# Turn-back of head pairs moved into the next period, one-hots of heads 3 to 11 placed by DMA, and a re-laid opening, in a routed-attention plus feed-forward kernel

## The chip, the cores and the metric

The kernel runs on one core of a Trainium2 chip. Times are device microseconds (us) of one execution. Kernels are compared only within the same rounds. A run that lies over 1.5% above the fastest of its kernel is called slow and left out.

## The reference

Attention in which a query sees only the keys that were assigned to the same one of 16 centroids, and then a feed-forward block without a nonlinearity:

```python
# B, H, S, D = 4, 8, 768, 64; 16 centroids per head
q_assign = argmax(normalise(q) @ normalise(centroids).T)      # k_assign likewise
mask     = q_assign[:, :, :, None] == k_assign[:, :, None, :]
scores   = where(mask, q @ k.T / 8, -1e9)
x        = softmax(scores) @ v                                # to [3072, 512]
out      = ((x @ w1) * (x @ w2)) @ w3 @ w_out
# ... (types, draws and reshapes cut)
```

## The kernel before

There are 32 heads (batch times head), each with its own *period*. Period p computes the scores and exponentials of head p, the value products of head p-1, and the preparation of head p+2. What is to be done in a period is a list of pairs (position, item), sorted by position and issued in that order; every engine then works through its own queue in order. Feed-forward work ("fill") is spread between these items. The kernel multiplies w3 by w_out once, so the fill has two kinds of products: up (`pu`) and down (`po`).

*Routing* of a head (`prr`) gives centroid scores, from which VectorE makes one-hots (`oh`). The one-hots are then transposed into PSUM (`pso`) and copied, 16 partitions at a time, into rows 64 to 79 of the head's transposed q and k (`xqk`), so that the score product applies the mask by itself. *Turn-back* (`join`): when both heads of a pair are done, their output (`xtm`) is transposed into PSUM (`psx`) and copied to `xT_all`, the feed-forward's input.

```python
psum_sc = tile_pool(name="psum_sc", bufs=3, space=PSUM)
psum_av = tile_pool(name="psum_av", bufs=1, space=PSUM)
psum_r  = tile_pool(name="psum_r",  bufs=1, space=PSUM)     # prr, pso, psx, pct: one bank in turn
psum_f  = tile_pool(name="psum_f",  bufs=3, space=PSUM)     # pst, pw, pu, po
# ...
    def route_turn(g, qeng=None):
        def item():
            pso = psum_r.tile([P, 3, P], BF16, name="pso", tag="r")
            for r in range(3):
                nc.tensor.transpose(out=pso[:, r], in_=oh[:, r]..., identity=ident)
            for a in (2, 0, 3, 1):
                dst = xqk[D : D + C, 3 * a : 3 * a + 3, :]
                src = pso[32 * a : 32 * a + C]
                # a < 2: a copy (VectorE, or qeng); else VectorE: src * MASKB - MASKB
# ...
    def join(g):
        xtm = xtm_cur[0]
        def item():
            psx = psum_r.tile([P, NCH, P], BF16, name="psx", tag="r")
            for sub in range(NCH):
                nc.tensor.transpose(out=psx[:, sub], in_=xtm[:, sub], identity=ident)
            nc.vector.tensor_copy(out=xT_all[:, h // 2, b * S : (b + 1) * S], in_=psx...)
# ...
        if 1 <= p and p + 2 < NG:
            work += [(0.36, route(p + 2)), (0.68, route_turn(p + 2))]
        if p >= 1:
            work += [(0.23 + 0.13 * i, it) for i, it in enumerate(av_items(p - 1))]
        if p >= 1 and (p - 1) % H % 2 == 1:
            work += [(0.93, lambda: join(p - 1)())]
# ...
        if p >= 1 and p % H == 0:      # a batch is complete: release its feed-forward items
```

The softmax here doesn't subtract the row's maximum and nothing guards it: scores larger than these inputs give would overflow.

## Time and profile before

| | before |
|---|---|
| median of the timed runs | 314.77 us (313.33 to 316.89) |
| span of the profiled run | 310.5 us |
| TensorE, ScalarE, VectorE, GpSimd busy | 92%, 66%, 59%, 34% |
| TensorE's waits of the turn-back on one-hot copies | 9.3 us in 14 waits |
| first score product | 15.04 us after the start |

In a timeline a line is: start, duration, engine, line, operation, what it writes and reads, count, and in brackets how long the engine had been idle and what ended it. The opening is seen in the following lines of the timeline of the kernel before (one-hots of head 0):

```profile
12.44 0.35 DVE L355 TENSOR_SCALAR xqk<-pso 16x384 bf16<-16x384 bf16 x1 [0.60 <-PE pso L343]
...
12.89 0.47 ACT L351 COPY xqk<-pso 16x384 bf16<-16x384 bf16 x1 [1.32 <-DVE xqk L355]
...
13.39 0.36 DVE L355 TENSOR_SCALAR xqk<-pso 16x384 bf16<-16x384 bf16 x1 [0.59 <-ACT xqk L351]
...
13.79 0.47 ACT L351 COPY xqk<-pso 16x384 bf16<-16x384 bf16 x1 [0.43 <-DVE xqk L355]
```

VectorE and ScalarE take turns on one bank; each starts when the other has ended.

### The profile page before, as it was taken

The page shows a single profiled execution, that of the slowest core. Times are in us where ns is not written, and L with a number is a line of the kernel's source. Part 1 is how long each engine was busy: PE and PEld are TensorE (multiplying, and loading weights), DVE is VectorE, ACT ScalarE, POOL GpSimd, SP SyncE. Part 2 cuts the span into 40 slices and gives each one's busy share as a digit, 9 for nine tenths or more (in the row PEclk, how much of TensorE's full clock was granted, in tenths as well). Part 3 has the DMA queues.
Part 4 walks back from the last instruction along what each step waited for, and adds up shares of the span by engine and source line. Part 5 has one row for each costly group of instructions (what it writes and reads, how often), then busy time and mean ns, then how long its engine had stood idle before and what let it go on. Part 6 is the DMA issues. An engine that isn't in the chain of part 4 may idle for free.

```text
span 310.5 us, 7304 instructions
## 1 busy us (share of the span) xinstructions
PE 286.6 (92%) x2972; PEld 172.1 (55%) x2972; DVE 183.6 (59%) x420; ACT 204.6 (66%) x369; POOL 104.7 (34%) x120
## 2 busy tenths in 40 slices
PE   5589898989799999999899999999999998999994
PEld 1447676655465656655565655555555555444441
DVE  4678798757676677655765465655666622342421
ACT  5667888755478888788677676867677776332330
POOL 1899875412633343073461047330300000000000
PEclk9657999999999999999999999999999999999999
DMA  7999997407555730879930689603910011002103
GB/s 188 290 252 229 264 261 170 70 0 141 141 137 135 148 106 0 173 196 229 199 106 12 162 222 225 158 0 100 243 25 2 1 70 68 2 0 101 36 0 136
DMA packets 52209, 38.78 MB, mean 125 GB/s; under 512 B 33744, under 2 KB 47056, under 8 KB 52176
## 3 DMA queue, kind: packets, MB, share of 16 engines
q1 hardware_dynamic: 48640, 32.88, 41.5%
q0 software_dynamic: 3392, 5.24, 9.9%
q8 instruction: 23, 0.38, 0.5%
q10 hardware_dynamic: 144, 0.20, 0.2%
q14 instruction: 10, 0.08, 0.1%
HBM read 29.39 MB, written 6.29 MB: 115 GB/s over the span
## 4 chain that ended last, share of the span: by engine, by line
PE 75%; DVE 13%; DMA 4%; ACT 3%; issue 2%; SPq 1%; DVEq 0%; ACTq 0%
PE pu L220 23%; PE po L239 13%; PE av L407 10%; PE sc L375 10%; PE sc L385 6%; PE pw L195 4%; DVE xqk L355 4%; DVE xqk L353 4%; PE prr L320 3%; PE psx L439 3%; PE pst L305 2%; DMA x_130<-in_k_dram 2%; DMA xqk<-stg 2%; PE pso L343 1%; ACT ex L379 1%
## 5 line engine op out<-in xcount | busy, mean ns | idle before, releaser
L379 ACT ACTIVATE ex<-sc 128x512 bf16<-128x512 f32 x192 | 111.8, 601 | 37.2 <-PE sc L375 36.2
L375 PE MATMUL sc<-xqk 80*128 80x512 bf16 x192 | 71.6, 390 | 0.3 <-ACT ex L379 0.2
L389 ACT ACTIVATE ex<-sc 128x512 bf16<-128x512 f32 x96 | 57.6, 600 | 19.6 <-PE sc L385 19.0
L228 DVE TENSOR_TENSOR ab<-pu,asb 128x512 bf16<-128x512 f32 x48 | 33.2, 692 | 42.5 <-PE pu L220 34.6
L407 PEld LDWEIGHTS <-ex 128*128 128x128 bf16 x1152 | 46.1, 98 | 10.3 <-ACT ex L379 0.4
L220 PE MATMUL pu<-xT_all,w1b 128*128 128x512 bf16 x192 | 49.4, 378 | 0.0
L220 PE MATMUL pu<-xT_all,w2b 128*128 128x512 bf16 x192 | 49.3, 378 | 0.0
L239 PE MATMUL po<-wc,ab 128*128 128x512 bf16 x192 | 47.0, 378 | 0.0
L226 ACT CAST asb<-pu 128x512 bf16<-128x512 f32 x48 | 28.1, 586 | 27.0 <-PE pu L220 26.8
L385 PE MATMUL sc<-xqk 80*128 80x256 bf16 x192 | 37.7, 278 | 0.4 <-ACT ex L389 0.2
L324 DVE TENSOR_REDUCE rsc<-prr 128x192 f32<-128x384 f32 x32 | 17.7, 554 | 27.1 <-PE prr L320 27.1
L239 PEld LDWEIGHTS <-ab 128*128 128x128 bf16 x192 | 18.5, 97 | 18.9
L220 PEld LDWEIGHTS <-w2b 128*128 128x128 bf16 x192 | 18.5, 97 | 18.8 <-issue 0.3
L220 PEld LDWEIGHTS <-w1b 128*128 128x128 bf16 x192 | 18.4, 97 | 18.5
L355 DVE TENSOR_SCALAR xqk<-pso 16x384 bf16<-16x384 bf16 x64 | 22.9, 358 | 5.3 <-PE pso L343 3.5
L385 PEld LDWEIGHTS <-xqk 80*128 80x128 bf16 x192 | 16.9, 100 | 13.2 <-issue 2.1
L353 DVE COPY xqk<-pso 16x384 bf16<-16x384 bf16 x62 | 21.7, 350 | 0.9
L375 PEld LDWEIGHTS <-xqk 80*128 80x128 bf16 x192 | 18.3, 99 | 6.4
L320 PEld LDWEIGHTS <-xqk 128*128 128x128 bf16 x384 | 14.8, 97 | 7.3 <-DVE xqk L309 1.8
L420 DVE TENSOR_TENSOR xtm<-av,rcp 128x384 bf16<-128x384 f32 x32 | 17.8, 558 | 1.1
L439 PE MATMUL psx<-ident,xtm 128*128 128x128 bf16 x96 | 8.1, 221 | 10.2 <-DVE xqk L353 9.3
L247 DVE COPY osb<-po 128x512 f32<-128x512 f32 x12 | 8.3, 692 | 15.4 <-PE po L239 15.2
(173 smaller groups left out, 348.5 us busy)
## 6 DMA issues: line engine op xcount, KB each, us to landing
out_dram<-osb SPq DMA_DIRECT2D x24, 256.0 KB, 2.1
w3b<-in_moe_w_dram POOLq DMA_DIRECT2D x8, 256.0 KB, 6.7
wob<-in_moe_w_out_dram POOLq DMA_DIRECT2D x4, 256.0 KB, 8.0
w1b<-in_moe_w_dram POOLq DMA_DIRECT2D x4, 256.0 KB, 6.6
w2b<-in_moe_w_dram POOLq DMA_DIRECT2D x4, 256.0 KB, 4.8
xqk<-stg SPq DMA_TRANSPOSE x20, 4.1
x_126<-in_q_dram ACTq DMA_DIRECT2D x1, 192.0 KB, 2.6
x_126<-in_k_dram SPq DMA_DIRECT2D x1, 192.0 KB, 2.7
```

The source lines that it names most:

```text
L220: nc.tensor.matmul(pu, lhsT=wb[:, fc, jc * P : (jc + 1) * P], rhs=xT_all[:, fc, t0 : t0 + TB], start=(fc == 0), stop=(fc == 3),)
L226: nc.scalar.copy(out=st["a"], in_=pu)
L228: nc.vector.tensor_tensor(out=st["ab"][:, jc], in0=pu, in1=st.pop("a"), op=ALU.mult)
L239: nc.tensor.matmul(st["o"], lhsT=st["ab"][:, jc, sub * P : (sub + 1) * P], rhs=wc[:, jc], start=(jc == 0), stop=(jc == 7),)
L320: nc.tensor.matmul(prr[:, j], lhsT=st["xqk"][:, j, :], rhs=cnt2[:, g % H], start=True, stop=True)
L353: nc.vector.tensor_copy(out=dst, in_=src)
L355: nc.vector.tensor_scalar(out=dst, in0=src, scalar1=MASKB, scalar2=-MASKB, op0=ALU.mult, op1=ALU.add,)
L375: nc.tensor.matmul(sc, lhsT=xqk[0:KR, NCH + 2 * pr + part, :], rhs=xqk[0:KR, 0:4, :], start=True, stop=True,)
L379: nc.scalar.activation(out=ex[:, part, 0:512], in_=sc, func=ACT.Exp, scale=SM_SCALE)
L385: nc.tensor.matmul(sc[:, i], lhsT=xqk[0:KR, NCH + 2 * pr + i, :], rhs=xqk[0:KR, 4:6, :], start=True, stop=True,)
L389: nc.scalar.activation(out=ex[:, :, 512:S], in_=sc, func=ACT.Exp, scale=SM_SCALE)
L407: nc.tensor.matmul(st["av"][:, sub, 0:VCOL], lhsT=st["exs"][j // 2][:, j % 2, sub * P : (sub + 1) * P], rhs=st["vb"][:, j, 0:VCOL], start= ...
```

## The change

Its intent: take the wait of the turn-back away by moving it to the next period, where the one-hot copies are long over; relieve VectorE of three of four copies for heads 3 to 11; and let the opening run through with a shorter chain, two banks for head 0's one-hots and a warmer TensorE.

```diff
-        for last in (False, True):          # two steps of the square root, now one
+        # ... one step (cut)
-        nc.scalar.copy(out=cnsrc[:, 1, D:P], in_=hi)
+        nc.vector.tensor_scalar_mul(out=cnsrc[:, 1, D:P], in0=cen, scalar1=rden)
 # cen_turn: its two transposes now in banks of psum_r and psum_f (cut)
+    def route_turn(g, split=False):
+        def direct():                       # head 0: split, two PSUM tiles, ScalarE beside VectorE
+            pso = ones_up(g, psum_r, "r")
+            psq = ones_up(g, psum_f, "f") if split else pso
+            # ... the four copies as before
+        def by_dma():
+            pso = ones_up(g, psum_r, "r")
+            ohT = rtp.tile([P, 3, P], BF16, name="ohT")
+            nc.vector.tensor_scalar(out=ohT, in0=pso, scalar1=msc[:, 0:1], scalar2=msc[:, 1:2],
+                                    op0=ALU.mult, op1=ALU.add)
+            for a in range(4):
+                nc.sync.dma_start(ones_rows(g, a), ohT[32 * a : 32 * a + C])
+        return by_dma if 3 <= g < PE_HEADS else direct
-        warm_up(10)
+        warm_up(13)
 # begin: order of cen_turn, turn_pe and low changed (cut)
-        route_turn(0, nc.scalar)()
+        warm_up(6)
+        route_turn(0, True)()
-            work += [(0.10, turn_pe(p + 2, 0)), (0.20, turn_pe(p + 2, 1))]
+            work += [(0.06, turn_pe(p + 2, 0)), (0.16, turn_pe(p + 2, 1))]
-            work += [(0.36, route(p + 2)), (0.68, route_turn(p + 2))]
+            work += [(0.45, route(p + 2)), (0.90, route_turn(p + 2))]
-        if p >= 1 and (p - 1) % H % 2 == 1:
-            work += [(0.93, lambda: join(p - 1)())]
+        if p % 2 == 1 and p >= 3:
+            work += [(0.25, join(p - 2))]
+        if p == NG:
+            work += [(0.95, join(p - 1))]
-        if p >= 1 and p % H == 0:
+        if (p > 1 and p % H == 1) or p == NG:
```

The last line follows from the move: a batch is complete one period later, so its feed-forward items are released one period later.

More of the change, by code (lines that the diff above doesn't have):

```diff
@@ L113 @@
     ident = const.tile([P, P], BF16, name="ident")
+    msc = const.tile([P, 2], F32, name="msc")
     ohs = [const.tile([P, 3, 4, 32], BF16, name=f"oh{i}") for i in range(3)]
@@ L124, in constants @@
             nc.vector.memset(oh, 0.0)
+        nc.vector.memset(msc[0 : P // 2, 0:1], 1.0)
+        nc.vector.memset(msc[0 : P // 2, 1:2], 0.0)
+        nc.vector.memset(msc[P // 2 : P, 0:1], MASKB)
+        nc.vector.memset(msc[P // 2 : P, 1:2], -MASKB)
         for vb in vbs:
@@ L136, in cen_norm @@
         nc.scalar.sqrt(nrm, ss)
-        for last in (False, True):
-            rr = setup.tile([P, 1], F32, name="rr")
-            nc.vector.reciprocal(out=rr, in_=nrm)
-            nrm2 = setup.tile([P, 1], F32, name="nrm2")
-            nc.vector.scalar_tensor_tensor(
-                out=nrm2, in0=ss, scalar=rr, in1=nrm, op0=ALU.mult, op1=ALU.add
-            )
-            nrm = setup.tile([P, 1], F32, name="nrm3")
-            nc.vector.tensor_scalar(
-                out=nrm, in0=nrm2, scalar1=0.5, scalar2=(1e-6 if last else 0.0),
-                op0=ALU.mult, op1=ALU.add,
-            )
+        rr = setup.tile([P, 1], F32, name="rr")
+        nc.vector.reciprocal(out=rr, in_=nrm)
+        twice = setup.tile([P, 1], F32, name="twice")
+        nc.vector.scalar_tensor_tensor(
+            out=twice, in0=ss, scalar=rr, in1=nrm, op0=ALU.mult, op1=ALU.add
+        )
+        den = setup.tile([P, 1], F32, name="den")
+        nc.vector.tensor_scalar(
+            out=den, in0=twice, scalar1=0.5, scalar2=1e-6, op0=ALU.mult, op1=ALU.add
+        )
         rden = setup.tile([P, 1], F32, name="rden")
-        nc.vector.reciprocal(out=rden, in_=nrm)
+        nc.vector.reciprocal(out=rden, in_=den)
         hi = cnsrc[:, 0, 0:D]
         nc.vector.tensor_scalar_mul(out=hi, in0=cen, scalar1=rden)
-        nc.scalar.copy(out=cnsrc[:, 1, D:P], in_=hi)
+        nc.vector.tensor_scalar_mul(out=cnsrc[:, 1, D:P], in0=cen, scalar1=rden)
         nc.vector.scalar_tensor_tensor(
@@ L161, in cen_turn @@
     def cen_turn():
-        pct = psum_r.tile([P, 2, P], BF16, name="pct", tag="r")
         for which in range(2):
-            nc.tensor.transpose(out=pct[:, which], in_=cnsrc[:, which, :], identity=ident)
-        for which in range(2):
+            pool, tag = ((psum_r, "r"), (psum_f, "f"))[which]
+            pct = pool.tile([P, P], BF16, name="pct", tag=tag)
+            nc.tensor.transpose(out=pct, in_=cnsrc[:, which, :], identity=ident)
             (nc.vector.tensor_copy, nc.scalar.copy)[which](
-                out=cnt2[:, :, :, which],
-                in_=pct[:, which].rearrange("p (h c) -> p h c", c=C),
+                out=cnt2[:, :, :, which], in_=pct.rearrange("p (h c) -> p h c", c=C)
             )
@@ L335, in route, with ones_up @@
         return item
-    def route_turn(g: int, qeng=None):
-        def item():
-            xqk = state[g]["xqk"]
-            oh = ohs[g % len(ohs)]
-            pso = psum_r.tile([P, 3, P], BF16, name="pso", tag="r")
-            for r in range(3):
-                nc.tensor.transpose(
-                    out=pso[:, r], in_=oh[:, r].rearrange("p a c -> p (a c)"), identity=ident
-                )
+    def ones_up(g: int, pool, tag):
+        oh = ohs[g % len(ohs)]
+        pso = pool.tile([P, 3, P], BF16, name="pso", tag=tag)
+        for r in range(3):
+            nc.tensor.transpose(
+                out=pso[:, r], in_=oh[:, r].rearrange("p a c -> p (a c)"), identity=ident
+            )
+        return pso
@@ L346, in item, with ones_rows, route_turn @@
+    def ones_rows(g: int, a: int):
+        return state[g]["xqk"][D : D + C, 3 * a : 3 * a + 3, :]
+    def route_turn(g: int, split: bool = False):
+        def direct():
+            pso = ones_up(g, psum_r, "r")
+            psq = ones_up(g, psum_f, "f") if split else pso
             for a in (2, 0, 3, 1):
-                dst = xqk[D : D + C, 3 * a : 3 * a + 3, :]
-                src = pso[32 * a : 32 * a + C]
                 if a < 2:
-                    if qeng is nc.scalar:
-                        nc.scalar.copy(out=dst, in_=src)
-                    else:
-                        nc.vector.tensor_copy(out=dst, in_=src)
+                    (nc.scalar.copy if split else nc.vector.tensor_copy)(
+                        out=ones_rows(g, a), in_=psq[32 * a : 32 * a + C]
+                    )
@@ L354, in item @@
                 else:
                     nc.vector.tensor_scalar(
-                        out=dst, in0=src, scalar1=MASKB, scalar2=-MASKB,
-                        op0=ALU.mult, op1=ALU.add,
-                    )
-        return item
+                        out=ones_rows(g, a), in0=pso[32 * a : 32 * a + C],
+                        scalar1=MASKB, scalar2=-MASKB, op0=ALU.mult, op1=ALU.add,
+                    )
+        def by_dma():
+            pso = ones_up(g, psum_r, "r")
+            ohT = rtp.tile([P, 3, P], BF16, name="ohT")
+            nc.vector.tensor_scalar(
+                out=ohT, in0=pso, scalar1=msc[:, 0:1], scalar2=msc[:, 1:2], op0=ALU.mult, op1=ALU.add
+            )
+            for a in range(4):
+                nc.sync.dma_start(ones_rows(g, a), ohT[32 * a : 32 * a + C])
@@ L393, in score_items @@
         return [item(pr, part) for pr in range(NCH // 2) for part in range(3)]
-    xtm_cur = {}
+    xtms = {}
     def av_items(g: int):
@@ L418, in it @@
                     if h % 2 == 0:
-                        xtm_cur[0] = xtmp.tile([P, NCH, P], BF16, name="xtm")
+                        xtms[g + 1] = xtmp.tile([P, NCH, P], BF16, name="xtm")
                     nc.vector.tensor_tensor(
-                        out=xtm_cur[0][:, :, (h % 2) * D : (h % 2) * D + D],
+                        out=xtms[g | 1][:, :, (h % 2) * D : (h % 2) * D + D],
                         in0=av[:, :, 0:D],
@@ L433, in join @@
         b, h = g // H, g % H
-        xtm = xtm_cur[0]
         def item():
+            xtm = xtms.pop(g)
             psx = psum_r.tile([P, NCH, P], BF16, name="psx", tag="r")
@@ L471, in begin @@
         low(0, 0, nc.vector)
+        cen_turn()
+        turn_pe(0, 0, "a")()
         low(0, 1, nc.vector)
-        turn_pe(0, 0, "a")()
-        cen_turn()
-        turn_pe(0, 1, "va")()
+        turn_pe(0, 1)()
         nc.scalar.activation(out=warm[:, 0:1], in_=warm[:, 0:1], func=ACT.Exp)
@@ L518, in in_period @@
         elif p == 1:
-            work += [(0.05, route_turn(2))]
+            work += [(0.02, route_turn(2))]
         if 1 <= p and p + 2 < PE_HEADS:
-            work += [(0.10, turn_pe(p + 2, 0)), (0.20, turn_pe(p + 2, 1))]
+            work += [(0.06, turn_pe(p + 2, 0)), (0.16, turn_pe(p + 2, 1))]
         if 1 <= p and p + 2 < NG:
-            work += [(0.36, route(p + 2)), (0.68, route_turn(p + 2))]
+            work += [(0.45, route(p + 2)), (0.90, route_turn(p + 2))]
         if p >= 1:
             work += [(0.23 + 0.13 * i, it) for i, it in enumerate(av_items(p - 1))]
-        if p >= 1 and (p - 1) % H % 2 == 1:
-            work += [(0.93, lambda: join(p - 1)())]
+        if p % 2 == 1 and p >= 3:
+            work += [(0.25, join(p - 2))]
+        if p == NG:
+            work += [(0.95, join(p - 1))]
         n = FILL(p, len(fill))
```

## The prediction

> **What bounds the kernel now.** I read the totals by engine first, then the waits, then the timeline around the longest wait of TensorE, then the busy times by stage. Totals, waits and transfer landings (a wait line is total us, times, longest):
>
> ```profile
> PE 286.6 (92%) x2972; PEld 172.1 (55%) x2972; DVE 183.6 (59%) x420; ACT 204.6 (66%) x369; POOL 104.7 (34%) x120
> ...
> PEld L439 <- DVE xqk L353: 15.8, 14, 2.1
> ...
> PE psx L439 <- DVE xqk L353: 9.3, 14, 1.7
> ...
> xqk<-stg SPq DMA_TRANSPOSE x20, 4.1
> ...
> cen<-in_centroids_dram SPq DMA_DIRECT2D x1, 32.0 KB, 2.4
> ```
>
> TensorE is busy for 92% of 310.5 us, so only 24 us of idle can be won. One cause holds 9.3 us of it: 14 times the transposes that turn a finished pair of heads back (psx) wait for VectorE to empty the one-hots (pso), because both use the single PSUM buffer of the routing pool. One such wait, from the timeline late in the kernel (start, duration, instruction, idle before it):
>
> ```profile
> 203.47 0.35 DVE L355 TENSOR_SCALAR xqk<-pso 16x384 bf16<-16x384 bf16 x1
> ...
> 203.84 0.35 DVE L353 COPY xqk<-pso 16x384 bf16<-16x384 bf16 x1
> 203.95 0.38 PE L375 MATMUL sc<-xqk 80*128 80x512 bf16 x1
> ...
> 204.20 0.36 DVE L355 TENSOR_SCALAR xqk<-pso 16x384 bf16<-16x384 bf16 x1
> 204.57 0.35 DVE L353 COPY xqk<-pso 16x384 bf16<-16x384 bf16 x1
> ...
> 204.98 0.34 PEld L439 LDWEIGHTS <-xtm 128*128 128x128 bf16 x6 [1.15 <-DVE xqk L353]
> 204.98 0.51 PE L439 MATMUL psx<-ident,xtm 128*128 128x128 bf16 x6 [0.65 <-DVE xqk L353]
> ```
>
> Four copies of 0.35 us run one after another and end at 204.92; psx starts 0.06 us later, after 0.65 us of idle TensorE. Busy times by stage (a period is the work between the first score products of two heads; the rows are heads 0, 1, 2, 3, and 24, 25):
>
> ```profile
> 15.04:22.86 7.82, 6.40 (x49) 3.64 (x46) 5.75 (x12) 4.83 (x9) 7.65 (x11) 0.50 1.00 249
> 22.86:29.57 6.71, 6.70 (x85) 5.09 (x84) 5.30 (x14) 4.01 (x8) 6.54 (x10) 0.71 1.00 213
> 29.57:36.46 6.89, 5.72 (x89) 4.10 (x89) 5.66 (x15) 6.05 (x11) 6.80 (x9) 1.00 1.13 275
> 36.46:42.01 5.55, 5.50 (x93) 4.32 (x91) 4.79 (x10) 4.43 (x10) 4.49 (x6) 1.00 1.17 264
> ...
> 197.34:206.41 9.07, 8.42 (x90) 4.97 (x89) 5.29 (x13) 7.03 (x13) 3.09 (x3) 1.00 0.17 56
> 206.41:214.32 7.91, 7.91 (x85) 4.72 (x84) 4.74 (x11) 5.55 (x10) 0.69 (x1) 1.00 0.10 35
> ```
>
> The columns are length, then busy time and count of PE, PEld, DVE, ACT, POOL, then granted clock, DMA share, GB/s. Even heads carry the turn-back and last longer (9.07 against 7.91, 6.89 against 5.55). In the odd ones TensorE is never idle, so they show the period that is left when the wait goes. The first two periods ran at half clock (0.50, 0.71), and DMA was at its full share up to head 3.
>
> **What the Trainium skill says.** "TensorE: Matmul & The Clock Gate", Part 1 (the HAM clock gate): the clock is halved until a free-running window of about 3.4 us was busy, and drops after an idle one. The trace agrees: the ten opening products come at 0.427 us each (512 columns at half rate), the clock record turns to 1.0 at 6.4 us, back to 0.5 at 9.8 and to 1.0 at 26.9. "PSUM — Partial Sum Buffer", bank collisions: two engines must not touch one bank and quadrant at once, so readers of one bank must be ordered. In the trace ScalarE and VectorE take turns on head 0's one-hots (12.44, 12.89, 13.39, 13.79), four copies in 1.82 us. "VectorE: DVE Perf Modes", errata section: a PSUM source costs 120 cycles plus the elements over the speed-up at 0.96 GHz, whatever the partitions; for 384 bf16 at 2x that is 0.33 us; the trace has 0.35 to 0.36 us for 16 x 384 and for 128 x 384. So one 128-partition copy costs what one 16-partition copy does. "DMA: Bandwidth & Descriptors", anatomy of one DMA: about 2 us are fixed; the smallest transfer here (32 KB) landed in 2.4 us.
>
> **The change, part by part.**
>
> 1. *Turn-back moved.* psx goes from position 0.93 of an even period to 0.25 of the next odd one, and the one-hots from 0.68 to 0.90. Between one-hots and psx there now lie, late in the kernel, two products groups of 0.86 us, three score products of 0.22 and one sixth of the values (0.41): 2.8 us. The four copies need about 0.5 + 1.42 = 1.9 us. The wait should vanish. Its worth: 9.3 us of recorded idle, and a bit more, since the end of a busy block includes the pipeline's tail. Late even minus odd is 9.07 - 7.91 = 1.16 us; the six transposes themselves take 0.34 (their weight loads), so the wait really cost 0.82 where 0.65 is recorded. 14 x 0.17 = 2.4; together 11.7 us. With only three fill items in periods 10 to 16 the distance is about 1.9 us, which is marginal; I take off 1.0. **-10.7.**
> 2. *One-hots of heads 3 to 11 by DMA.* Nine times four copies (1.42 us) become one copy (0.36) and four transfers: 9 x 1.06 = 9.5 us less on VectorE, which does not bound; worth nothing by itself. The cost is a new latency. Copy and wait 1.0 us, four issues at some 0.4 us = 1.6, landing 2.4: 5.0 to 5.8 us, against 1.1 periods to the head's first product, 6.1 us at 5.5 us per period. It just fits; for heads 3, 4, 5 and 10 (whose periods are short) I allow a little. The queue is in order, so loads of inputs from head 6 on now also wait for these transfers: head 6's load moves from 15 us to about 28, needed prepared at about 37, with 3 us to land and 3 us of GpSimd (0.84 + 1.64 + 0.50): hidden by some 3 us. **+0.7.**
> 3. *Opening.* One square-root step less (0.16 + 0.22 + 0.15 and gaps, 0.64 us), the centroid copy off ScalarE, the one-hots of head 0 in two banks (saves about 0.9). Against it, six warming products ahead of head 0's one-hots: 6 x 0.427 = 2.6 us at half clock, starting about 9.7, done 12.2, while the one-hots should be ready at 11.4. And head 1's two copies, not head 0's, released the first score product at 15.04. Net **-0.4**.
> 4. *Clock.* 13 + 6 warming products should bring the full clock at some 13 us instead of 26.9. Heads 0 and 1 at full clock would last some 6.3 (then VectorE's chain, 5.75 busy) and 5.6 us: -2.2. But the window's phase is not ours; I take two thirds: **-1.5.**
> 5. *Fill moved.* The product work of a batch is released one period later: period 9 gets none, period 31 gets 5 instead of 2. Period 9 keeps about 4.9 us of TensorE work against nine exponentials at about 0.5 us: little lost, **+0.3**. In period 31 TensorE waited on exponentials (0.22 + 0.29 us idle) and is now covered: **-0.5.** The wait of the last turn-back (0.9 us) stays.
>
> Sum: -10.7 + 0.7 - 0.4 - 1.5 + 0.3 - 0.5 = -12.1. From the median of 315.3: **303.2 us**.
>
> **Rivals.** (a) *The DMA of the one-hots comes late*, and the head's first score product waits in place of psx. For it: DMA share is 1.0 until 42 us, transfers of 192 KB took 6 to 8 us to land there, 5.8 against 6.1 us is no margin. Against: input loads are now held back, so their queue is empty by then. Up to 9 waits of 1 us: 312 us. (b) *ScalarE becomes the bound early.* For it: 6.05 of 6.89 us in head 2. Against: its records overlap (0.60 us each, 0.5 apart), odd head 3 with the same work lasts 5.55. It would take 2 us of the gain: 305. (c) *Input loads held by the in-order queue* starve GpSimd's preparation in heads 4 to 8: a few us, 306 to 308. (d) *The clock stays at half* and the six warming products only delay: +0.9 + 1.5, 305.6.
>
> **Range and chances.** The main term is firm, as odd periods already run without the wait; (a) and (c) can eat half, the clock can give 1 more. The three runs before differ by 3.6 us. Range 298.5 to 309; the 2% line is at 309.0. Faster 0.88, same 0.10, slower 0.02.
>
> **What would show it.** Right: no wait of psx on VectorE beyond the last one; even and odd late periods 8.1 and 8.2 us, equal within 0.3; the granted clock at 1.0 from some 13 us; the first score product at 14.6; the first products of heads 3 to 11 not waiting for DMA. Wrong: a row in which score weights or products wait for the one-hot transfers or the turn-back still waits for the pso copies; half clock up to 25 us; preparation on GpSimd waiting for inputs in heads 6 to 8 and TensorE waiting for it; the even and odd periods equal but both nearer 9 us, which would mean that the wait had hidden something else.

## The result, and the profile after

The changed kernel takes 304.77 us at the median (303.42 to 306.23), against 314.77. The ratio is 0.968, 95% interval 0.959 to 0.976. Such a ratio is the mean time of one kernel's fast runs over that of the other's of the same rounds, so it is not quite the ratio of the medians. The prediction had 303.2 us. The result is correct.

The totals and the remaining waits of the turn-back (psx), from the page and the waits of the kernel after:

```profile
PE 283.5 (93%) x2948; PEld 172.8 (57%) x2984; DVE 178.0 (59%) x395; ACT 202.1 (66%) x367; POOL 103.4 (34%) x120
...
PE psx L456 <- DVE xqk L359: 1.6, 3, 0.6
...
PE psx L456 <- DVE xtm L437: 1.2, 1, 1.2
...
PE pwarm L471 <- ACT warm L493: 1.1, 1, 1.1
...
PEld L392 <- DMA xqk<-ohT: 0.5, 1, 0.5
```

Fourteen waits of 9.3 us in all became three of 1.6 us in all. (Of the 2984 matmuls that the weight loads count, 36 have no record here, so TensorE's 283.5 us are a little low.) Two new lines have appeared: the warming products waited for ScalarE, and a head's scores for a transfer of one-hots. Late in the kernel the timeline shows what was intended:

```profile
198.31 0.36 DVE L363 TENSOR_SCALAR xqk<-pso 16x384 bf16<-16x384 bf16 x1
198.68 0.35 DVE L359 COPY xqk<-pso 16x384 bf16<-16x384 bf16 x1
...
199.71 0.35 PEld L456 LDWEIGHTS <-xtm 128*128 128x128 bf16 x6
199.74 0.50 PE L456 MATMUL psx<-ident,xtm 128*128 128x128 bf16 x6
```

The last copy ends at 199.03; psx comes 0.71 us later, with no idle in brackets. The stages, with the same columns as in the prediction; heads 0, 1, 2, 3, and 25, 26:

```profile
16.68:24.71 8.03, 5.20 (x48) 3.32 (x45) 6.13 (x12) 4.73 (x9) 7.86 (x11) 0.79 0.70 117
24.71:30.07 5.36, 5.10 (x87) 4.03 (x84) 4.57 (x12) 4.02 (x8) 3.83 (x5) 1.00 0.82 135
30.07:35.10 5.03, 4.92 (x84) 3.98 (x83) 3.90 (x10) 4.73 (x10) 0.00 (x0) 1.00 0.43 77
35.10:41.49 6.39, 5.78 (x97) 4.71 (x97) 4.31 (x11) 5.64 (x11) 4.33 (x5) 1.00 0.62 186
198.06:206.30 8.24, 8.18 (x90) 5.06 (x90) 6.08 (x14) 6.44 (x13) 5.39 (x5) 1.00 0.39 104
206.30:214.20 7.90, 7.84 (x83) 4.71 (x83) 4.47 (x11) 6.00 (x11) 0.51 (x1) 1.00 0.10 36
```

The late pair takes 16.14 us instead of 16.98. Its two periods differ by 0.34 us, the six transposes. But the first row begins at 16.68: the first score product comes 1.64 us later than before, although the opening was meant to be shorter. These are two single executions; the table below has more of each opening.

### The profile page after: what moved, and what is told of

Same layout as the page of the kernel before. It is cut to its first block, busy times and chain, and to the rows that moved or that the text cites.

```text
span 304.2 us, 7357 instructions
## 1 busy us (share of the span) xinstructions
PE 283.5 (93%) x2948; PEld 172.8 (57%) x2984; DVE 178.0 (59%) x395; ACT 202.1 (66%) x367; POOL 103.4 (34%) x120
## 4 chain that ended last, share of the span: by engine, by line
PE 80%; DVE 8%; ACT 5%; DMA 4%; issue 2%; SPq 0%; DVEq 0%
PE pu L223 25%; PE po L242 13%; PE sc L392 12%; PE av L424 11%; PE sc L402 5%; PE pw L198 4%; PE prr L323 3%; ACT ex L396 2%; DMA x<-in_q_dram 2%; DVE oh L331 2%; PE pst L308 2%; PE psx L456 2%; PE pso L344 2%; DMA xqk<-ohT 1%; ACT ex L406 1%
## 5 line engine op out<-in xcount | busy, mean ns | idle before, releaser
L424 PEld LDWEIGHTS <-ex 128*128 128x128 bf16 x1152 | 47.0, 97 | 13.5 <-issue 1.5
L424 PE MATMUL av<-vb,ex 128*128 128x65 bf16 x1152 | 51.7, 193 | 0.2
L291 POOL TENSOR_TENSOR stg<-x,stg 128x768 bf16<-128x768 f32 x30 | 49.4, 1646 | 2.5
L290 POOL CAST stg<-x 128x768 bf16<-128x768 f32 x30 | 24.9, 832 | 72.4 <-DMA x<-in_k_dram 50.9
L223 PE MATMUL pu<-xT_all,w1b 128*128 128x512 bf16 x179 | 47.4, 378 | 0.7
L223 PE MATMUL pu<-xT_all,w2b 128*128 128x512 bf16 x183 | 47.5, 378 | 0.5
L242 PE MATMUL po<-wc,ab 128*128 128x512 bf16 x184 | 45.1, 378 | 0.4
L285 POOL CAST vb<-x 128x384 bf16<-128x384 f32 x32 | 16.7, 521 | 32.1 <-PE av L424 24.9
L402 PEld LDWEIGHTS <-xqk 80*128 80x128 bf16 x192 | 16.9, 98 | 11.0 <-issue 0.5
L363 DVE TENSOR_SCALAR xqk<-pso 16x384 bf16<-16x384 bf16 x46 | 16.5, 358 | 7.4 <-PE pso L344 6.7
L331 DVE TENSOR_TENSOR oh<-rsc,mx 128x192 bf16<-128x192 f32 x32 | 18.3, 573 | 1.1
```

Of the source, the lines that this page charges most:

```text
L223: nc.tensor.matmul(pu, lhsT=wb[:, fc, jc * P : (jc + 1) * P], rhs=xT_all[:, fc, t0 : t0 + TB], start=(fc == 0), stop=(fc == 3),)
L242: nc.tensor.matmul(st["o"], lhsT=st["ab"][:, jc, sub * P : (sub + 1) * P], rhs=wc[:, jc], start=(jc == 0), stop=(jc == 7),)
L290: nc.gpsimd.tensor_copy(out=stg[:, :, 0:D], in_=qk32)
L291: nc.gpsimd.tensor_tensor(out=stg[:, :, D:P], in0=qk32, in1=stg[:, :, 0:D], op=ALU.subtract)
L331: nc.vector.tensor_tensor(out=oh[:, :, :, 0:C].rearrange("p r a c -> p a r c"), in0=rsc.rearrange("p (a r) c -> p a r c", r=3), in1=mx.rea ...
L402: nc.tensor.matmul(sc[:, i], lhsT=xqk[0:KR, NCH + 2 * pr + i, :], rhs=xqk[0:KR, 4:6, :], start=True, stop=True,)
```

## The experiments

All eleven runs below, with the two kernels above, were taken apart by the same five stages of their profiles: start of the first score product, heads 0 and 1, heads 2 to 9, 10 to 16, 17 to 30, and the rest (times in us). The fill is not placed alike: kernels with the moved turn-back have three fill items fewer in heads 2 to 9, two fewer in 17 to 30, and five more in the rest. One item is four products of 0.216 us, so 0.86 us. To compare, add 2.6 and 1.7 to the two stages of those kernels and take 4.3 off the rest.

| kernel | first | 0-1 | 2-9 | 10-16 | 17-30 | rest | median | ratio to before (95%) |
|---|---|---|---|---|---|---|---|---|
| before | 15.04 | 14.53 | 62.74 | 46.23 | 117.47 | 54.5 | 314.77 | 1 |
| after | 16.68 | 13.39 | 56.07 | 48.57 | 111.31 | 58.2 | 304.77 | 0.968 (0.959-0.976) |
| after2 (same) | 16.47 | 13.24 | 56.64 | 46.21 | 111.30 | 58.2 | 304.23 | 0.968 (0.962-0.974) |
| joinonly | 15.93 | 13.24 | 57.06 | 46.99 | 111.32 | 58.0 | 306.54 | 0.970 (0.967-0.974) |
| openonly | 15.68 | 13.03 | 64.54 | 46.23 | 117.67 | 54.4 | 314.56 | 0.997 (0.994-0.9995) |
| nodma | 16.47 | 13.24 | 56.71 | 46.99 | 111.31 | 58.1 | 304.54 | 0.969 (0.965-0.973) |
| psxf | 16.29 | 14.39 | 59.21 | 44.52 | 113.24 | 54.4 | 305.44 | 0.968 (0.964-0.972) |
| dry | 15.50 | 13.24 | 60.09 | 47.14 | 111.31 | 58.2 | 304.12 | 0.971 (0.966-0.976) |
| own | 13.65 | 15.10 | 56.09 | 48.03 | 111.31 | 58.2 | 304.66 | 0.969 (0.965-0.973) |
| split | 16.52 | 12.21 | 56.85 | 45.94 | 111.31 | 58.2 | 303.39 | 0.966 (0.962-0.969) |
| best1 | 14.38 | 15.28 | 56.54 | 47.42 | 111.31 | 58.2 | 304.98 | 0.969 (0.965-0.973) |
| afterf | 17.27 | 13.26 | 56.34 | 45.79 | 111.31 | 58.2 | 303.86 | 0.967 (0.961-0.973) |
| best2 | 14.50 | 15.59 | 59.71 | 44.52 | 110.97 | 55.3 | 302.17 | 0.960 (0.954-0.965) |

The stage from head 17 on repeats to 0.02 us between executions of kernels with the moved turn-back; the ones before it move by one or two us. Heads 10 to 16 move only in kernels with transfers of one-hots; without them they repeat to 0.01 us (before and openonly, joinonly and nodma, psxf and best2). The opening moves too: the same instructions gave a first score product at 15.04, 15.93 and 16.29 us (before, joinonly, psxf), and the changed opening 15.68 to 17.27 (after, after2, openonly, nodma, split, afterf). (The 64.54 of openonly holds a stretch of half clock in head 9, which took 8.47 us instead of 6.85.) The kernel before had medians of 314.64 to 315.44 us.

### Does the moved turn-back alone give the gain? (joinonly)

```diff
 # the kernel before, with only these of the change
+            work += [(0.45, route(p + 2)), (0.90, route_turn(p + 2))]
+        if p % 2 == 1 and p >= 3:
+            work += [(0.25, join(p - 2))]
+        if (p > 1 and p % H == 1) or p == NG:      # release
 # ... (xtms in place of xtm_cur, the 0.02 and 0.06/0.16 positions)
```

> The kernel before with the turn-back moved alone: turn-back at 0.25 of the next period, routing at 0.45 and one-hots at 0.90, products of a batch released one period later; opening and one-hot copies as before. Theory (the move is nearly the whole gain): 305.5 to 307 us against 314.6, ratio 0.970 to 0.976; heads 17 to 30 at 111.3 us as in the changed kernel (117.47 before), heads 2 to 9 at 56.7, first score product at 15.0 as before. Rival (much of the gain came from the opening and the clock): ratio over 0.98.

Measured: ratio 0.970, so 3.0% of the 3.2%; heads 17 to 30 at 111.32. The move is nearly the whole gain, and the rival falls. In heads 10 to 16 it lost 0.8 us instead of gaining: three waits of 0.55 us of the turn-back, in heads 11, 13 and 15, stay. I had expected the first score product at 15.0 as before; with the same opening it came at 15.93, so that stage moves by about 1 us by itself.

### Is the opening worth anything? (openonly)

```diff
 # the changed kernel with the periods of the kernel before and all one-hots copied directly
+            work += [(0.36, route(p + 2)), (0.68, route_turn(p + 2))]
+        if p >= 1 and (p - 1) % H % 2 == 1:
+            work += [(0.93, join(p - 1))]
 # ... (the other positions, the release and "return direct": cut)
```

> The changed kernel with the periods and the one-hots of the kernel before, so that only the opening differs from it (one square-root step less, two banks for head 0, 13 + 6 warming products). Theory: the first score product later by 1 to 1.7 us, heads 0 and 1 shorter by 0.5 to 2 us for the earlier clock, together within 1 us of the kernel before, ratio 0.997 to 1.003. Rival (the opening is worth the 1.9 us that was predicted for opening and clock together): ratio 0.994 or lower.

Measured: ratio 0.997 (0.994 to 0.9995): about 1 us, at the edge of what can be told from nothing, and half of the 1.9 us that was predicted for opening and clock. (With every run of both kernels, slow ones too, the means are in the ratio 0.998.) The product of the two parts, 0.9704 x 0.9968 = 0.9673, agrees with the whole change's 0.968: within the noise the parts add.

### Is the transfer of one-hots worth anything? (nodma)

```diff
-        return by_dma if 3 <= g < PE_HEADS else direct
+        return direct
```

> The changed kernel with the one-hots of heads 3 to 11 copied by VectorE into place as before, four copies each. Theory (VectorE is off the path there, the transfers are hidden): within 1 us of the changed kernel, heads 2 to 9 at 56 us as there (56.07), the input loads issued early again (head 6 at about 15 us instead of 33). Rival (the DMA is what shortens heads 2 to 9, as VectorE's queue was what held the turn-back and the copies): heads 2 to 9 longer by 2 us or more, waits of the turn-back on the one-hot copies coming back there.

Measured: 0.969 against 0.968, heads 2 to 9 at 56.71 against 56.07 and 56.64 in the changed kernel's two profiles. The nine times 1 us that VectorE was spared buy nothing that shows. The profile also has the issues of head 6's loads at 14.9 us instead of 33.8, so the in-order queue did hold the loads back, even longer than the predicted 28 us. In the time that is hidden. In heads 9 to 16 it shows: with the transfers GpSimd waits there for inputs (1.1 to 8.1 us, five times in the changed kernel), without them never in nodma and joinonly.

### Is it the shared PSUM buffer or the place in the period? (psxf)

```diff
 # the kernel before; nothing moved
-            psx = psum_r.tile([P, NCH, P], BF16, name="psx", tag="r")
+            psx = psum_f.tile([P, NCH, P], BF16, name="psx", tag="f")
```

> The kernel before with the turn-back's PSUM tile taken from the pool of the feed-forward products (three buffers) instead of the routing pool's single one, nothing moved. Theory (the wait is for the shared buffer alone): TensorE's waits of the turn-back on the one-hot copies (9.3 us) vanish at the old place too, heads 17 to 30 fall from 117.47 to about 112.9 (the 14 products of four that are counted in the later release stay, so not to 111.3), ratio 0.970 to 0.98. Rival (VectorE's queue is the limit, the turn-back's copy only comes after the others): a new wait of the products on the turn-back's copy, and half of the gain or less.

Measured: 305.44 us, ratio 0.968, the same as the whole change and a little better than I had expected. The same place in the timeline as the prediction's, in the profile of psxf:

```profile
197.54 0.35 DVE L355 TENSOR_SCALAR xqk<-pso 16x384 bf16<-16x384 bf16 x1
...
197.91 0.35 DVE L353 COPY xqk<-pso 16x384 bf16<-16x384 bf16 x1
198.03 0.38 PE L375 MATMUL sc<-xqk 80*128 80x512 bf16 x1
198.03 0.54 PEld L439 LDWEIGHTS <-xtm 128*128 128x128 bf16 x6
...
198.25 0.50 PE L439 MATMUL psx<-ident,xtm 128*128 128x128 bf16 x6
198.28 0.36 DVE L355 TENSOR_SCALAR xqk<-pso 16x384 bf16<-16x384 bf16 x1
...
198.65 0.35 DVE L353 COPY xqk<-pso 16x384 bf16<-16x384 bf16 x1
```

psx starts while VectorE still has two of the four copies to make. The rival, that VectorE's queue would only hand the wait on, falls: the products show no new wait there (in the whole profile one wait of 0.32 us on the turn-back's copy is listed, early, at 50.33 us). The stage from head 17 falls to 113.24 us, 111.5 when its two further fill items are taken off. Heads 10 to 16 take 44.52 us, less than in any kernel with the moved turn-back. "Perfetto Trace Analysis" of the Trainium skill, Optimizing Tensor Performance, advises that independent matmul groups rotate through different PSUM banks so that emptying one overlaps the next; this run shows the advice worth 9.7 us of 315.

### Why is the first score product late? (dry and own)

The opening in the timeline of the changed kernel:

```profile
11.47 0.21 ACT L493 ACTIVATE warm<-warm 128x1 bf16<-128x1 bf16 x1
11.70 0.62 DVE L331 TENSOR_TENSOR oh<-rsc,mx 128x192 bf16<-128x192 f32 x1
11.73 2.33 PE L471 MATMUL pwarm<-warm 128*128 128x512 bf16 x6 [1.05 <-ACT warm L493]
...
13.86 0.85 PE L344 MATMUL pso<-ident,oh 128*128 128x128 bf16 x6
```

The six warming products read the tile `warm`, and the preload of the exponential's table writes one column of it. So they wait until 11.73, not 9.7 as I had assumed, and the one-hots, ready at 12.32, wait until 13.86. Of the 1.64 us by which this execution's first score product is later than before, 0.47 had arisen earlier: in the kernel before the one-hots were ready at 11.85.

```diff
 # dry
-        warm_up(6)
 # own
+    pre = const.tile([P, 1], BF16, name="pre")
-        nc.scalar.activation(out=warm[:, 0:1], in_=warm[:, 0:1], func=ACT.Exp)
+        nc.scalar.activation(out=pre, in_=warm[:, 0:1], func=ACT.Exp)
```

> The changed kernel without the six warming products ahead of head 0's one-hots. Theory (they delay the opening: they wait for the preload of the exponential, which writes the same tile, and then take 2.3 us at half clock): the first score product at 14.9 to 15.3 us instead of 16.68, head 0's one-hots turned at about 12.4 instead of 13.86. Rival (they bring the full clock): the granted clock stays at half for longer, up to 25 us, heads 0 and 1 take over 14 us instead of 13.4, and the time is equal or longer than the changed kernel's. If only the delay counts, 1.4 us faster than the changed kernel; if both count, within 1 us of it.

> The changed kernel with the exponential's preload writing a tile of its own, so that the six warming products do not wait for it. Theory: they start right after head 0's routing products at about 10.7 us instead of 11.73, end at about 13.0, head 0's one-hots are turned at about 13.0 instead of 13.86, the first score product at 15.8; about 0.8 us faster than the changed kernel, with the same clock. Rival (the wait of TensorE on ScalarE is only how the profile names it): no change of these times.

Measured, dry: one-hots turned at 12.57 and the first score product at 15.50 us, 1.2 earlier. The rival (they bring the full clock) is half right: the granted clock stayed at half from 11.01 to 21.25 us, while in the six profiles with these products it turned to full at 13.5 to 16.9. But heads 0 and 1 take 13.24 us, no longer than with them. The time is the changed kernel's. In the profile (of the slowest of the six runs, 307.44 us) two heads now wait for their one-hots; head 6's wait in the timeline of dry:

```profile
52.46 0.48 DVE L371 TENSOR_SCALAR ohT<-pso,msc 128x384 bf16<-128x384 bf16 x1 [0.16 <-DMA xqk<-ohT]
52.97 3.18 SPq L375 DMA_DIRECT2D xqk<-ohT  x4
...
54.69 0.09 PEld L392 LDWEIGHTS <-xqk 80*128 80x128 bf16 x1 [2.33 <-DMA xqk<-ohT]
54.69 0.39 PE L392 MATMUL sc<-xqk 80*128 80x512 bf16 x1 [2.05 <-DMA xqk<-ohT]
```

Head 6 stands 2.05 us, head 3 another 1.16, and heads 2 to 9 take 60.09. Right behind it the granted clock fell to half for 3.4 us (0.60 on average from 54.69 to 58.00). Such waits appear in five further profiles: 1.75 us in split, 0.92 in best1, 0.44 in afterf, 0.41 in after2, 0.2 in after. None is in nodma and joinonly, which have no such transfers. The rival (a) of the prediction is thus real, but comes and goes between executions.

Measured, own: the six products start at 9.41 us right behind the routing and end before the one-hots are ready, so the wait on ScalarE was real. They ran at full clock (1.46 us instead of 2.33), and the first score product came at 13.65, better than expected; 1.1 us of that had arisen before them, as the routing began at 9.10 instead of 10.21. Then the granted clock was only 0.59 in head 0 and 0.75 in head 1 (15.10 us together), and the gain was gone. Neither run is faster than the changed kernel beyond the noise.

### Why did heads 10 to 16 lose 2.3 us? (split and after2)

In the timeline of the changed kernel, during the period of head 10 (GpSimd's cast and subtraction, VectorE's comparison, TensorE's transposes of the result):

```profile
89.26 0.83 POOL L290 CAST stg<-x 128x768 bf16<-128x768 f32 x1 [8.14 <-DMA x<-in_k_dram]
...
90.17 1.64 POOL L291 TENSOR_TENSOR stg<-x,stg 128x768 bf16<-128x768 f32 x1
90.38 1.65 DVE L331 TENSOR_TENSOR oh<-rsc,mx 128x192 bf16<-128x192 f32 x1
...
92.08 0.34 PE L344 MATMUL pso<-ident,oh 128*128 128x128 bf16 x3 [0.60 <-DVE oh L331]
```

The comparison takes 0.36 us in most periods. Here it was issued 0.21 us behind a subtraction and ended 0.22 us after it. "SBUF — State Buffer" of the Trainium skill, Who interferes with whom, says that a VectorE instruction with two SBUF inputs contends with a GpSimd instruction that reads SBUF. That is this pair. All 13 profiles bear it out: 150 comparisons began while a cast or subtraction of GpSimd had more than 0.15 us left, and every one of them ended 0.19 to 0.24 us after it; of the 205 that met neither, 201 took 0.36 us.

```diff
-        nc.gpsimd.tensor_tensor(out=stg[:, :, D:P], in0=qk32, in1=stg[:, :, 0:D], op=ALU.subtract)
+        for i in range(0, NC2, 3):
+            nc.gpsimd.tensor_tensor(out=stg[:, i : i + 3, D:P], in0=qk32[:, i : i + 3],
+                                    in1=stg[:, i : i + 3, 0:D], op=ALU.subtract)
```

> The changed kernel with GpSimd's subtraction of a head (1.64 us) in four pieces. Theory (VectorE's one-hot comparison, which has two inputs in SBUF, is held while GpSimd's operation runs): the comparisons of heads 10 and 12 fall from 1.65 us to at most 0.9, TensorE's waits on them (0.60 us each) and on the last one-hot copy in heads 11 and 13 shrink, heads 10 to 16 take 46.5 to 47.8 us instead of 48.57; 0.7 to 2 us faster in all. Rival (something else slows them, the order of VectorE's queue or the transfers): 1.65 us stays and the time is the same or longer by GpSimd's added overheads.

> The changed kernel once more, unaltered, as the control of this call. All theories: ratio to the kernel before 0.965 to 0.971. In its profile heads 10 to 16 should again take over 47.5 us with one-hot comparisons of 0.9 us and more in them, if that loss is the kernel's and not the one execution's.

Measured, split: no comparison of heads 10 to 16 is over 0.76 us, the stage takes 45.94 us, TensorE's idle in it falls from 2.85 to 0.56 us. Shorter GpSimd pieces hold VectorE for less, as expected. But the control, after2, with nothing altered, took 46.21 us: one comparison of 1.15 us, one of 0.73, and the rest at 0.36. So the loss of 2.3 us is not fixed by the kernel, as I had expected, but differs with how GpSimd and VectorE happen to meet. It is not of one execution alone either: own, with the same code in this stage, lost 1.8 us against the 46.23 of the kernel before (comparisons of 1.71 and 1.06 us) and dry 0.9 (one of 1.50). What all these share are the transfers of one-hots, behind which the input loads come late and GpSimd starts when they land, as in the first line above; in nodma and joinonly GpSimd never waits here, five comparisons of 0.92 us meet its cast each time, and the stage takes 46.99 us in both. Whether split is faster than the changed kernel (0.966 against 0.968) can't be told.

### Does the shared bank still matter at the new place? (afterf)

```diff
 # the changed kernel
-            psx = psum_r.tile([P, NCH, P], BF16, name="psx", tag="r")
+            psx = psum_f.tile([P, NCH, P], BF16, name="psx", tag="f")
```

> The changed kernel with the turn-back's PSUM tile taken from the feed-forward pool. Theory (the shared buffer is what made the turn-back wait at its new place in heads 11, 13 and 15 as well): the three waits of 0.55 us are gone and heads 10 to 16 fall from 48.57 to 46 to 47; heads 17 to 30 stay at 111.3. If it was VectorE's held comparison alone, 48 or more. In all 0 to 2 us faster than the changed kernel.

Measured: no wait of psx on the copies is left, and heads 10 to 16 take 45.79 us, 0.4 less than the control in the same rounds, which is less than this stage moves. In all 0.967 against 0.968: inconclusive in time.

### A first version of everything (best1)

```diff
 # split and own, warm_up(3), and
+        if p + 2 < PE_HEADS:      at = (0.42, 0.76) if p % 2 else (0.36, 0.70)
+        elif p <= 2 * H:          at = (0.55, 0.90)
+        else:                     at = (0.45, 0.90)
+        work += [(at[0], route(p + 2)), (at[1], route_turn(p + 2))]      # (shortened)
+            work += [(0.30 if 10 <= p <= 16 else 0.25, join(p - 2))]
```

> The changed kernel with all that the runs so far point to: GpSimd's subtraction in four pieces, the exponential's preload off the warming tile, three warming products instead of six, one-hots of heads 3 to 11 earlier in their period (0.70 or 0.76), the turn-back at 0.30 and the routing at 0.55 in periods 10 to 16. Theory: no wait of score products on the one-hot transfers, heads 10 to 16 at 45.5 us or less, first score product at 13.7 to 15, 301.5 us at the median, 1.5 to 3 us faster than the changed kernel. Rival (the clock's phase decides): within 1 us of it.

Measured: 304.98 us, a miss. Head 3 still waited 0.92 us for its transfer. With the routing nearer to the one-hots, TensorE waited for the comparison instead: 0.39 to 0.73 us in heads 3, 5, 9, 10 and 12. Heads 10 to 16 take 47.42. Shifting positions only traded one wait for another.

### The version that the runs point to (best2)

```diff
 # the kernel before, with the changed kernel's opening, and
-            psx = psum_r.tile([P, NCH, P], BF16, name="psx", tag="r")
+            psx = psum_f.tile([P, NCH, P], BF16, name="psx", tag="f")
-        nc.scalar.activation(out=warm[:, 0:1], in_=warm[:, 0:1], func=ACT.Exp)
+        nc.scalar.activation(out=pre, in_=warm[:, 0:1], func=ACT.Exp)
-        warm_up(6)
+    if p == 2 * H + 1:      # fill of period 17: three items, so that some are left for period 31
+        return 3
```

> The kernel before with three alterations: the turn-back's PSUM tile from the feed-forward pool, the changed kernel's opening without its six late warming products and with the preload off the warming tile, and three products items instead of five in period 17, so that two are left for period 31. Theory (the gains add): heads 10 to 16 at 44.5 us, heads 17 to 30 at 111.5, no wait on transfers of one-hots; 302 to 304 us, ratio 0.960 to 0.967, 0.5 to 2 us faster than the changed kernel. Rival (the opening gives nothing): 0.968 as with the buffer alone.

Measured: 302.17 us (300.37 to 303.15), ratio 0.960. All six runs are below the fastest of the control's six (303.18). It beats both kernels, without moving the turn-back and without a single transfer of one-hots. No share of the further 2 us was measured by itself, but the profiles of psxf and best2 can be laid side by side. Up to head 10 both need the same time (89.89 and 89.80 us): the first score product comes 1.8 us earlier in best2, but its clock stayed at half until 28.44 us, heads 0 and 1 take 1.2 us more and heads 2 to 9 another 0.5, and the gain of the opening is gone. Heads 10 to 16 take 44.52 us in both. From head 17 on, with the same work in sum, best2 takes 166.3 us instead of 167.65. So the 1.4 us between these two executions lie where the fill was moved, not in the opening.

## Why the prediction was right or wrong

The time (304.77 against 303.2), the range and the direction were right. Measured one by one, the parts give -9.3 us (move and fill, joinonly), -1.0 (opening and clock, openonly) and nothing clear (transfers, nodma), where -10.9, -1.9 and +0.7 were predicted. By its steps:

1. *Turn-back moved, -10.7 predicted.* Right in mechanism. joinonly, which holds this part and step 5, gained 0.0296 x 315.1 = 9.3 us against 10.9 predicted for the two. Late the size is right to half a us: the wait plus 0.17 us each was worth 4.9 us by the prediction's working in heads 17 to 30, and 117.47 - 111.31 - 1.7 = 4.5 was measured. In heads 10 to 16 I took off 1.0 us for a distance that I called marginal; that was too little. Three waits of 0.55 us stayed in joinonly, and the stage lost 0.8 us where 0.7 was to be gained. In heads 2 to 9 the gain was 62.74 - 57.06 - 2.6 = 3.1 in joinonly and 4.1 in the changed kernel, against 5.1: ScalarE's exponentials now end some of the waits there (0.25 us in heads 3 to 5), a milder form of rival (b). (The "one sixth of the values" between one-hots and psx is a third: 12 products of 36. The distance of 2.8 us was right: 196.80 to 199.74.)
2. *One-hots by DMA, +0.7.* Right in kind: worth nothing, with a margin that is too thin now and then. Two sizes were off: an issue took 0.54 us, not 0.4, and the one 128-partition copy 0.48, not 0.36. Landing took 1.7 to 6.6 us around 2.8. Rival (c), loads held by the in-order queue, came true in a small way: the late loads go with the scatter of heads 10 to 16, as above.
3. *Opening, -0.4.* The sign was wrong in the profile, +1.6 us at the first score product; over the executions of both openings it is about +0.8 (means 15.75 and 16.52 us), with ranges that overlap. The step that failed is "starting about 9.7": the six warming products wait for the preload of the exponential, which writes their tile. The timeline of before had this preload at 11.37 us, `ACTIVATE warm<-warm`; the prediction does not take it up. The two banks for head 0 saved 0.5 us (four copies in 1.33 instead of 1.82), not 0.9. The four copies read partitions from 64, 0, 96 and 32 on, so four quadrants: the section that the prediction cites on bank collisions does not ask them to take turns. What ordered them isn't shown; all four read one tile.
4. *Clock, -1.5.* Half right. (The clock's records in the kernel before stand at 6.25, 9.67 and 26.73 us, 0.15 before the prediction's.) The six products do bring the full clock sooner, at 13.5 to 16.9 us (15.60 in the changed kernel) instead of 22.0 to 27.5 in the three profiles of the old opening, but in four of the six it was lost again for 3.4 us (here from 19.01). Heads 0 and 1 took 12.2 to 13.4 us against 13.2 to 14.5: about 1 us, but the ranges overlap. own and best1, with nearly the same opening, took 15.1 and 15.3. openonly puts steps 3 and 4 together at about -1.0 us (interval -1.9 to -0.2), against -1.9.
5. *Fill moved, -0.2 in sum.* The wait on exponentials in period 31 is gone as foretold; the last turn-back's wait stayed (1.16 us).

What the prediction did not ask was whether the wait could be had more cheaply. It named the cause, the single PSUM buffer, and then priced only the move away from it. psxf shows that the cause itself could be taken away by one word.

It stays open how much of best2's further gain the fill of period 17 brings over many executions, and what sets the clock's phase. The mean granted clock of a run cannot tell: it takes the time before the first record of the clock as full. psxf's profile has a mean of 0.998, yet its first record is the turn to full at 27.52 us, and its score products last longer before it than after:

```profile
25.15 0.63 PE L375 MATMUL sc<-xqk 80*128 80x512 bf16 x1
...
28.04 0.38 PE L375 MATMUL sc<-xqk 80*128 80x512 bf16 x1
```

So a mean near 1 can stand for a whole opening at half clock (psxf) or for a good one (split, 0.994, full from 4.27 us but for 3.4 us). Of joinonly's six runs, those at 0.998 and 0.999 took 306.6 to 306.7 us and the one at 0.976 took 304.57.

## What to carry to other kernels

When the bounding engine waits for a buffer that an unrelated tile still holds, first give the tile another bank and only then move work about; a pool with slack may already be there. Moving work to where the wait would be over gains as much where the distance is ample, and loses where it is marginal. A filler instruction is only free if it depends on nothing: look at every writer of the tile that it reads. And before explaining a stage of one profile, look at the same stage in a second execution.

## What the Trainium skill lacked or had wrong

- "VectorE: DVE Perf Modes", errata: 120 cycles plus elements over the speed-up gives, as an estimate, 0.33 us at 2x or 0.53 us at 1x for 384 elements from PSUM. The scale and offset of 128 x 384 with per-partition values from SBUF took 0.468 to 0.478 us in nine of nine, neither of the two; with constants, on 16 partitions, 0.358. The section has no term for per-partition values.
- "DMA: Bandwidth & Descriptors", anatomy of one DMA: the fixed 2 us is given for the path through GpSimd. SBUF-to-SBUF transfers of 12 KB from the Sync queue landed in 1.7 us at best, 2.8 to 3.6 at the median and 5.1 to 7.2 at worst in seven profiles, and cost 0.54 us of issue each. No spread is stated there, and here it decided whether a head waited.
- "SBUF — State Buffer", who interferes with whom: right. What the runs add is how it looks in a profile: not as idle, but as a longer VectorE record (1.65 us in place of 0.36), which ended 0.19 to 0.24 us after GpSimd's in 150 of 150 cases.
- "TensorE: Matmul & The Clock Gate", Part 1: right that the phase is free. Six profiles of the same opening gave 6.6 to 8.0 us for head 0. The runs add that a wait can cost more than its length: behind idle stretches of TensorE of 2.05 us (dry) and 1.66 us (openonly, at the end of head 8) the granted clock went to half for 3.4 us; behind the same 1.66 us in the kernel before it did not. The page lets the clock drop after an idle window of about 3.4 us and gives no share of busy time; in the 3.4 us before these two drops TensorE was busy for 40% and 51%, and in the kernel before, without a drop, for 51%.
